# Scores with the keys on the partitions, exp straight from PSUM without the row maximum, row sums from a ones column beside V, and a flagged general path

## The chip, the cores and the metric

One core of one Trainium2 chip runs the program. The metric is device time in microseconds for one execution. TensorE is PE in the profile (PEld is its weight load), VectorE is DVE, ScalarE is ACT, GpSimd is POOL and SyncE is SP.

## The reference

One block of a conditioned transformer: attention with a cached K and V, then a gated MLP that mixes along the sequence. Sizes: 2048 rows, width 512, 32 query heads over 8 K/V heads (4 query heads share one), 2048 keys, head width 128, MLP width 2 x 896.

```python
mod = (silu(c) @ w_mod)                  # six rows of 512: sa, ca, ga, sb, cb, gb
h = layernorm(x) * (1 + ca) + sa
q = h @ wq                               # 32 heads of 128
scores = q k^T * 128 ** -0.5             # per head 2048 x 2048
o = softmax(scores) @ v
x = x + ga * (o @ wo)
h = layernorm(x) * (1 + cb) + sb
z = gelu(h @ w_in)                       # z1 = z[:, :896], z2 = layernorm(z[:, 896:])
g = w_sp @ z2 + b_sp                     # along the sequence, w_sp is 2048 x 2048
x = x + gb * ((z1 * g) @ w_out)
```

The inputs are normal numbers times 0.05; `wq` is scaled down once more by 512 ** -0.5.

## The kernel before

**Set-up (L82 to L219).** SP issues every load: x, c, w_mod and, for each K/V head g, `wq`, V, K and `wo` (`load_group`, L129). 24 columns and two rows of the modulation are made with small matmuls (L163, L189). Everything of K, V, `wq` and `wo` stays in SBUF. K is turned on PE (`kbuild`, L103).

**Attention (L221 to L389).** The loops run over 16 query tiles j of 128 rows, 8 heads g and 4 query heads hh: 512 steps. `prepare_qtile` (L224) normalizes and turns one query tile, `qproj` (L252) makes the four heads' queries of a group with 16 matmuls of 128 columns. A step has two halves:

- `stage1` (L273). Queries on the partitions: four matmuls 128x512 make a row block of scores 128 x 2048 in two PSUM tiles `s_ps` (L280). DVE scales each half out of PSUM into `s_sb` in bf16 and takes the row maximum on the way (L287), then joins the two maxima (L297). ACT takes the exp of the whole 128 x 2048 block with the negated maximum as bias and gives the row sum (L300); DVE inverts it (L309). Then the block of probabilities must have its keys on the partitions, so SP issues one DMA transpose of 128 x 2048 (L321): `pT3`.
- `stage2` (L324), one step later: 16 matmuls of 128 columns with `pT3` as the weights and V as the moving operand (L327), ACT scales the result by the inverse sum (L335), PE turns it (L336).

After the four heads, `group_end` (L338) multiplies by `wo` with four matmuls of 512 columns (L343); after the eight groups, `qtile_end` (L351) adds into x and takes the statistics of the second layer norm. The order is written out by hand with `pending` (L361 on): the next group's `qproj`, then `stage1` of a step, then `stage2` of the step before.

**MLP.** The first half (L437 on) goes by row tile: normalize, turn on PE (L455), shift and scale on ACT (L460), 16 matmuls of 448 columns (L470), then GELU as six instructions on ACT and DVE with a sigmoid (L478 to L499), and statistics (L503). In the same loop SP issues 16 DMA transposes of `w_sp` (L447). When all statistics are there, z2 is normalized (L519). The second half (L531 on) goes by row tile: 32 matmuls of 448 columns (L535), bias on ACT (L543), product on DVE (L551), 7 turns on PE (L559), 7 matmuls with `w_out` (L564), two DVE instructions (L572, L574) and the store (L575).

Of the kernel before, what the change touches and what calls it, by code (L numbers as in the profile page):

```python
# [10 lines left out]
BF16 = mybir.dt.bfloat16  # L11
FP32 = mybir.dt.float32
ACT = mybir.ActivationFunctionType
ALU = mybir.AluOpType
AX = mybir.AxisListType
P = 128
LN_EPS = 1e-5
# [3 lines left out]
def _f_chunk(f: int) -> int:  # L21
    for cand in range(512, 0, -1):
        if f % cand == 0:
            return cand
    return 1


@with_exitstack
def kernel(
    ctx: ExitStack,  # L30
    tc: tile.TileContext,
    A_x: bass.AP,
# [9 lines left out]
    c: bass.AP,  # L42
    w_mod: bass.AP,
    out: bass.AP,
    stage: str = "full",
):
    nc = tc.nc
    _, S, D = A_x.shape
    _, HKV, SK, DH = A_k_cache.shape
    HQ = A_wq.shape[1] // DH  # L50
    REP = HQ // HKV
    F = B_w_in.shape[1]
    FH = F // 2
    NMOD = w_mod.shape[1]
    assert DH == P and D % P == 0 and S % P == 0 and SK % 1024 == 0 and FH % P == 0
    assert D <= 512 and NMOD == 6 * D and REP * P <= 512
    NT = S // P
    NDT = D // P
    NKT = SK // P
    NKH = SK // 1024  # L60
    NFT = FH // P
    FC = _f_chunk(FH)
    NFHC = FH // FC
    NFC = 2 * NFHC
    inv_sqrt_dh = 1.0 / math.sqrt(DH)
    NPE_STEPS = 0

    x_dram = A_x[0].rearrange("(t p) d -> p t d", p=P)
    out_dram = out[0].rearrange("(t p) d -> p t d", p=P)
# [22 lines left out]
    with tc.tile_pool(name="psum_att", bufs=1, space=bass.MemoryType.PSUM) as psum_att, tc.tile_pool(  # L92
        name="attres", bufs=1
# [6 lines left out]
        mv1 = attres.tile([P, NT, nc.vector.BN_AGGR_DIM], FP32, name="mv1")  # L100
# [20 lines left out]
        with tc.tile_pool(name="setup", bufs=1) as setup:  # L121
            wmod_sb = setup.tile([P, NDT, NMOD], BF16, name="wmod_sb")
            c_bf = setup.tile([P, NDT], BF16, name="c_bf")
# [24 lines left out]
            c_f = setup.tile([P, NDT], FP32, name="c_f")  # L148
            nc.vector.tensor_copy(out=c_f[:], in_=c_bf[:])
            sig = setup.tile([P, NDT], FP32, name="sig")  # L150
            nc.scalar.activation(out=sig[:], in_=c_f[:], func=ACT.Sigmoid)
            sc = setup.tile([P, NDT], FP32, name="sc")
            nc.vector.tensor_tensor(out=sc[:], in0=c_f[:], in1=sig[:], op=ALU.mult)
            sc_bf = setup.tile([P, NDT], BF16, name="sc_bf")
            nc.vector.tensor_copy(out=sc_bf[:], in_=sc[:])
            ones_bf = setup.tile([P, P], BF16, name="ones_bf")
            nc.vector.memset(ones_bf[:], 1.0)
            for i in range(6):
                for dt in range(NDT):
                    col = i * NDT + dt  # L160
                    mc_ps = psum_att.tile([P, D], FP32, name="X_ps")
                    for kt in range(NDT):
                        nc.tensor.matmul(  # L163
                            mc_ps[:, 0:1],
                            lhsT=wmod_sb[:, kt, i * D + dt * P : i * D + (dt + 1) * P],
                            rhs=sc_bf[:, kt : kt + 1],
                            start=(kt == 0),
                            stop=(kt == NDT - 1),
                        )
                    nc.vector.tensor_copy(out=modc[:, col : col + 1], in_=mc_ps[:, 0:1])  # L170
            for i in (1, 4):
                nc.vector.tensor_scalar_add(
                    out=modc[:, i * NDT : (i + 1) * NDT],
                    in0=modc[:, i * NDT : (i + 1) * NDT],
                    scalar1=1.0,
                )
            lhs_list = []
            for kt in range(NDT):
                lhs_bc = setup.tile([P, P], BF16, name=f"lhs_bc{kt}")
                nc.vector.tensor_scalar_mul(  # L180
                    out=lhs_bc[:], in0=ones_bf[:], scalar1=sc[:, kt : kt + 1]
                )
                lhs_list.append(lhs_bc)
            for row_out, i in ((ga_rows, 2), (gb_rows, 5)):
                for nch in range((D + 511) // 512):
                    nsz = min(512, D - nch * 512)
                    mr_ps = psum_att.tile([P, D], FP32, name="X_ps")
                    for kt in range(NDT):
                        nc.tensor.matmul(  # L189
                            mr_ps[:, :nsz],  # L190
                            lhsT=lhs_list[kt][:],
                            rhs=wmod_sb[:, kt, i * D + nch * 512 : i * D + nch * 512 + nsz],
                            start=(kt == 0),
# [26 lines left out]
        with tc.tile_pool(name="qpool", bufs=2) as qpool, tc.tile_pool(  # L220
# [130 lines left out]
            def qtile_end(X_ps, j):  # L351
                xa = qpool.tile([P, D], FP32, name="xa")
                nc.vector.tensor_tensor(out=xa[:], in0=X_ps[:], in1=ga_rows[:], op=ALU.mult)
                nc.vector.tensor_tensor(out=x_sb[:, j, :], in0=xa[:], in1=x_sb[:, j, :], op=ALU.add)
                stats2 = qpool.tile([P, 1, nc.vector.BN_STATS_DIM], FP32, name="stats2")
                nc.vector.bn_stats(out=stats2[:, 0, :], in_=x_sb[:, j, :])
                nc.vector.bn_aggr(out=mv2[:, j, :], in_=stats2[:])
                if stage == "attn":
                    nc.sync.dma_start(out=out_dram[:, j, :], in_=x_sb[:, j, :])

            pending = None  # L361
            for j in range(NT):
# [27 lines left out]
            stage2(pg, phh, ppT3, prinv, poT_view)  # L390
            group_end(pX_ps, pg, poT_view)
            qtile_end(pX_ps, pj)

    if stage == "attn":
        return

    with tc.tile_pool(name="mres", bufs=1) as mres:
        win_sb = mres.tile([P, NDT, F], BF16, name="win_sb")
# [176 lines left out]
                nc.sync.dma_start(out=out_dram[:, tt, :], in_=yout[:])  # L575


# [1 line left out]
_INS = ['A_x', 'A_k_cache', 'A_v_cache', 'A_wq', 'A_wo', 'B_x', 'B_w_in', 'B_w_sp', 'B_b_sp', 'B_w_out', 'c', 'w_mod']  # L579
_OUTS = [((1, 2048, 512), 'bfloat16')]  # L580
# [25 lines left out]
```

## Time and profile before

| | |
|---|---|
| median of 3 runs | 2018.55 us (2013.92 to 2029.61) |
| span of the profiled execution, first to last instruction | 2017.7 us |
| median less that span | 0.9 us |
| PE busy, share of the span | 1548.8 us, 77% |
| DVE busy | 1531.4 us, 76% |
| ACT busy | 1384.9 us, 69% |
| DMA queue of SP: share of 16 engines | 83.6% |
| packets on it | 1149168, 303.77 MB |
| read from HBM | 24.78 MB |

The profile comes from one execution. For the profiled execution no time is listed beside its span, so the span stands for it. "Busy" of PE counts pipelined matmuls whose ends are modelled: the distance from the start of one line to the start of the next says more than the mean duration. A group line gives its source line, engine, operation and tile, the shapes, the count, busy time and mean of one instruction, then the idle time of the engine just before and what ended it. A line of the timeline gives start, length, engine, source line, operation, tiles and count; several equal instructions in a row are merged. SPq lines are issues of transfers; their length is the time that the issuing takes.

### The profile page before, as it was taken

What the parts mean: (1) busy time and instruction counts of PE and PEld (TensorE: products, weight loads), DVE (VectorE), ACT (ScalarE), POOL (GpSimd) and SP (SyncE); (2) the same over time, 40 slices, a digit from 0 to 9 for tenths busy, and PEclk for the clock granted to TensorE, in tenths of its full rate; (3) what the DMA queues carried; (4) which work ended last, traced back from release to release, by engine and by line L of the source; (5) the groups of instructions that cost most, each with busy time, mean ns of one, the idle gap of its engine ahead of it and who ended that gap; (6) DMA issues with size and microseconds to landing.
All of it is one profiled execution on the core that took longest, in us unless ns stands there. A gap on an engine that the chain in (4) does not pass through costs nothing. (4 is left out here: it accounts for less than half of the span.)

```text
span 2017.7 us, 36999 instructions
## 1 busy us (share of the span) xinstructions
PE 1548.8 (77%) x14664; PEld 958.1 (47%) x14664; DVE 1531.4 (76%) x3634; ACT 1384.9 (69%) x1804; POOL 1.2 (0%) x8
## 2 busy tenths in 40 slices
PE   4478788878777877777777777777777787756898
PEld 2355455545444545445454555445544554423344
DVE  5478888888878887888777887887888887769422
ACT  1467778777777777777777776777777787768222
POOL 0000000000000000000000000000000000000000
PEclk9799999999999999999989999998999999989899
DMA  9989989999989998999989998988999999990000
GB/s 300 226 142 159 168 161 171 169 160 165 163 152 163 169 162 157 163 157 159 157 142 162 165 160 139 172 151 149 166 158 164 159 173 151 168 209 13 11 17 16
DMA packets 1149342, 306.13 MB, mean 152 GB/s; under 512 B 1134448, under 2 KB 1147632, under 8 KB 1149168
## 3 DMA queue, kind: packets, MB, share of 16 engines
q1 hardware_dynamic: 1149168, 303.77, 83.6%
q8 instruction: 114, 1.87, 0.3%
q14 instruction: 60, 0.49, 0.1%
HBM read 24.78 MB, written 2.10 MB: 13 GB/s over the span
## 5 line engine op out<-in xcount | busy, mean ns | idle before, releaser
L287 DVE TENSOR_SCALAR_CACHE_REDUCE s_sb<-s_ps 128x1024 bf16<-128x1024 f32 x1024 | 1228.4, 1217 | 288.9 <-PE s_ps L280 261.8
L300 ACT ACTIVATE p_sb<-s_sb,nm 128x2048 bf16<-128x2048 bf16 x512 | 1021.7, 1996 | 110.6 <-DVE nm L297 37.1
L327 PE MATMUL o_ps<-v_sb,pT 128*128 128x128 bf16 x8192 | 561.8, 223 | 281.3 <-DMA pT<-p_sb 279.3
L327 PEld LDWEIGHTS <-pT 128*128 128x128 bf16 x8192 | 485.7, 100 | 422.1 <-DMA pT<-p_sb 394.6
L280 PE MATMUL s_ps<-kT_sb,qT 128*128 128x512 bf16 x2048 | 613.6, 388 | 58.9 <-DVE s_sb L287 55.2
L335 ACT ACTIVATE onorm<-o_ps,rinv 128x128 bf16<-128x128 f32 x512 | 184.6, 361 | 322.2 <-PE o_ps L327 320.4
L280 PEld LDWEIGHTS <-qT 128*128 128x128 bf16 x2048 | 178.4, 100 | 131.5 <-issue 78.6
L258 PE MATMUL qT_ps<-hT,wq_sb 128*128 128x128 bf16 x2048 | 174.9, 220 | 5.4 <-ACT qT L266 4.4
L258 PEld LDWEIGHTS <-wq_sb 128*128 128x128 bf16 x2048 | 139.1, 98 | 60.8 <-issue 17.2
L336 PE MATMUL oT_ps<-ident,onorm 128*128 128x128 bf16 x512 | 117.0, 229 | 38.0 <-ACT onorm L335 27.6
L336 PEld LDWEIGHTS <-onorm 128*128 128x128 bf16 x512 | 49.8, 97 | 191.6 <-ACT onorm L335 179.9
L343 PE MATMUL X_ps<-wo_sb,oT 128*128 128x512 bf16 x512 | 135.2, 387 | 2.1 <-DVE oT L340 1.1
L535 PE MATMUL g_ps<-z_sb,wspT_sb 128*128 128x448 bf16 x512 | 103.8, 356 | 12.9 <-DVE z_sb L519 12.9
L300 ACT ACTIVATION_READ_ACCUMULATOR p_sb<-s_sb,nm 128x1 f32 x512 | 96.8, 189 | 0.0
L309 DVE RECIPROCAL rinv<-rs 128x1 f32<-128x1 f32 x512 | 80.9, 158 | 12.1 <-ACT p_sb L300 9.3
L266 ACT ACTIVATE qT<-qT_ps 128x512 bf16<-128x512 f32 x128 | 75.6, 590 | 20.9 <-PE s_ps L280 11.0
L287 DVE DVE_READ_ACCUMULATOR s_sb<-s_ps 128x1 f32 x1024 | 84.4, 82 | 0.0
L340 DVE COPY oT<-oT_ps 128x512 bf16<-128x512 bf16 x128 | 53.9, 421 | 32.8 <-PE oT_ps L336 32.2
L535 PEld LDWEIGHTS <-wspT_sb 128*128 128x128 bf16 x512 | 49.6, 98 | 59.7 <-issue 15.9
L343 PEld LDWEIGHTS <-oT 128*128 128x128 bf16 x512 | 46.2, 99 | 63.6 <-DVE oT L340 16.9
L297 DVE TENSOR_REDUCE nm<-mh 128x1 f32<-128x2 f32 x512 | 73.5, 143 | 3.6
L470 PE MATMUL zpre_ps<-win_sb,h2T 128*128 128x448 bf16 x256 | 53.5, 364 | 28.3 <-ACT xs L478 27.9
(121 smaller groups left out, 481.6 us busy)
## 6 DMA issues: line engine op xcount, KB each, us to landing
pT<-p_sb SPq DMA_TRANSPOSE x512, 4.5
wq_sb<-in_A_wq_dram SPq DMA_DIRECT2D x8, 512.0 KB, 5.9
v_sb<-in_A_v_cache_dram SPq DMA_DIRECT2D x8, 512.0 KB, 7.3
kT_sb<-in_A_k_cache_dram SPq DMA_DIRECT2D x8, 512.0 KB, 8.5
wo_sb<-in_A_wo_dram SPq DMA_DIRECT2D x8, 512.0 KB, 6.0
x_sb<-in_A_x_dram SPq DMA_DIRECT2D x1, 2048.0 KB, 8.4
wmod_sb<-in_w_mod_dram SPq DMA_DIRECT2D x1, 2048.0 KB, 9.3
out_dram<-yout SPq DMA_DIRECT2D x16, 128.0 KB, 1.7
```

The source lines that it names most:

```text
L258: nc.tensor.matmul(qT_view[:, hh, :], lhsT=wq_sb[:, dt, h * DH : (h + 1) * DH], rhs=hT[:, dt, :], start=(hh == 0 and dt == 0), stop=(hh == ...
L266: nc.scalar.activation(out=qT[:], in_=qT_view, func=ACT.Copy)
L280: nc.tensor.matmul(s_ps[:, c2 * 512 : (c2 + 1) * 512], lhsT=qT[:, hh, :], rhs=kT_sb[:, g, kc * 512 : (kc + 1) * 512], start=True, stop=True,)
L287: nc.vector.tensor_scalar(out=s_sb[:, hf * 1024 : (hf + 1) * 1024], in0=s_ps[:], scalar1=inv_sqrt_dh, scalar2=None, op0=ALU.mult, op1=ALU.max,
L297: nc.vector.tensor_reduce(out=nm[:], in_=mh[:], axis=AX.X, op=ALU.max, negate=True)
L300: nc.scalar.activation(out=p_sb[:], in_=s_sb[:], func=ACT.Exp, bias=nm[:], scale=1.0, accum_out=rs[:],)
L309: nc.vector.reciprocal(out=rinv[:], in_=rs[:])
L327: nc.tensor.matmul(o_ps[:], lhsT=pT3[:, kt, :], rhs=v_sb[:, g, kt, :], start=(kt == 0), stop=(kt == NKT - 1),)
L335: nc.scalar.activation(out=onorm[:], in_=o_ps[:], func=ACT.Copy, scale=rinv[:])
L336: nc.tensor.transpose(oT_view[:, hh, :], onorm[:], ident[:])
L343: nc.tensor.matmul(X_ps[:], lhsT=oT[:, hh, :], rhs=wo_sb[:, h, :], start=(h == 0), stop=(h == HQ - 1),)
L535: nc.tensor.matmul(g_ps[:, ch, :FC], lhsT=wspT_sb[:, st, tt * P : (tt + 1) * P], rhs=z2_sb[:, st, ch * FC : (ch + 1) * FC], start=(st == 0 ...
```

## The change

The old kernel function becomes `general_path`, unchanged but for a debugging switch. A new one runs first:

- **Units.** Four chunks of 512 rows, in each the 8 groups; a unit is one group for 128 rows of queries, all four heads together: 128 units. K, V, `wq` and `wo` of a group are loaded a group ahead into double buffers, so each comes from HBM four times. K is turned by a DMA transpose on its way in.
- **Scores turned.** The weights are a block of 128 keys, the moving operand is the 4 x 128 queries of the unit: a matmul 128x512 gives 128 keys by 512 scores. Two of them fill one `s_ps`, 128 x 1024 in fp32, of which there are two.
- **No maximum.** ACT takes the exp from PSUM into `pT` in bf16, which has its keys on the partitions already. No DVE instruction stands between.
- **Sums.** V has a column of ones (`v1`, 130 wide, 129 used); 16 matmuls of 129 columns give a head's output and its sum. DVE inverts the sums and scales two heads at a time.
- **Output.** One DMA transpose 128 x 512 per unit turns the four heads' outputs for `wo`.
- **Order.** `for it`: eight slots; in each the scores of unit `it` (two matmuls), the products with V of unit `it-1` (eight), and one matmul of `qproj` for the next group (slots 0 to 3) or of `wo` for unit `it-2` (slots 4 to 7).
- **MLP.** GELU is one ACT instruction; z1 is made transposed; the mixing works on turned blocks, 16 matmuls of 512 columns per block, so nothing is turned on PE. `w_sp` is loaded with 64 DMA transposes of 512 x 128, the first 32 issued right ahead of the units.
- **Flag.** If an inverse sum lies outside 2^-60 to 2^60, a flag is set; at the end every engine reads it, and `general_path` runs only if it is not zero.

The set-up's queue order is as the diff has it: SP also carries c and the first four tiles of x ahead of the K turns. `ln1_norm` issues four DMA transposes on SP; after `mod_columns` of the last four parts come the two rows ga and gb (8 matmuls of 512 columns). In the MLP each chunk of 512 rows has 32 matmuls of 448 columns and 28 of 512, each group of four followed by one GELU, and later 7 x 16 with `w_sp` and 4 x 7 with `w_out`.

The diff, cut to its core (`general_path` is the kernel shown above):

```diff
+    def load_wsp(t):
+        for st in range(NT):
+            nc.sync.dma_start_transpose(
+                out=wsp[t][:, st, :],
+                in_=B_w_sp[t * 512 : (t + 1) * 512, st * P : (st + 1) * P],
+            )
...
+        def load_group(n):
...
+            g = n % HKV
+            kT = kvp.tile([P, SK], BF16, name="kT")
+            nc.sync.dma_start_transpose(out=kT[:], in_=A_k_cache[0, g])
+            v1 = kvp.tile([P, NKT, DV], BF16, name="v1")
+            nc.gpsimd.memset(v1[:, :, DH:DV], 1.0)
+            nc.gpsimd.dma_start(out=v1[:, :, 0:DH], in_=v_dram[:, g])
...
+            nc.gpsimd.dma_start(out=wo_g[:], in_=wo_dram[:, g * REP : (g + 1) * REP, :])
+            groups[n] = dict(kT=kT, v1=v1, wo=wo_g)
...
+            nc.scalar.dma_start(out=wmod_sb[:, :, 0 : 2 * D], in_=wmod_dram[:, :, 0 : 2 * D])
+            wqs[0] = load_wq(0)
+            load_group(0)
+            nc.scalar.dma_start(
+                out=wmod_sb[:, :, 2 * D : NMOD], in_=wmod_dram[:, :, 2 * D : NMOD]
+            )
+            wqs[1] = load_wq(1)
+            load_group(1)
+            for t in range(1, NCH):
+                nc.sync.dma_start(
+                    out=x_sb[:, t * CT : (t + 1) * CT, :],
+                    in_=x_dram[:, t * CT : (t + 1) * CT, :],
+                )
+            nc.sync.dma_start(out=win_sb[:], in_=win_dram)
+            nc.sync.dma_start(out=wout_sb[:], in_=wout_dram)
+            nc.sync.dma_start(out=bsp_bc[:], in_=B_b_sp.partition_broadcast(P))
...
+            mod_columns((0, 1))
...
+            ln1_mod(0, ln1_norm(0))
...
+            for hh in range(REP):
+                for f in qproj(0, hh):
+                    f()
+
+            mod_columns((2, 3, 4, 5))
...
+        for t in range(2):
+            wsp[t] = wspp.tile([P, NT, 512], BF16, name=f"wsp{t}")
+            load_wsp(t)
...
+        def qk(u, i):
...
+            s_ps = psum.tile([P, 1024], FP32, name="s_ps", bufs=2)
+            for h in range(2):
+                kt = 2 * i + h
+                nc.tensor.matmul(
+                    s_ps[:, h * 512 : (h + 1) * 512].rearrange("p (r q) -> p r q", r=REP),
+                    lhsT=groups[n]["kT"][:, kt * P : (kt + 1) * P],
+                    rhs=qTs[n][:, :, jj * P : (jj + 1) * P],
+                    start=True,
+                    stop=True,
+                )
+            nc.scalar.activation(
+                out=pTs[u][:, 2 * i : 2 * i + 2, :],
+                in_=s_ps[:].rearrange("p (k q) -> p k q", k=2),
+                func=ACT.Exp,
+                scale=inv_sqrt_dh,
+            )
...
+            for kt in range(part * NKT // per, (part + 1) * NKT // per):
+                nc.tensor.matmul(
+                    o_ps[:, hh % 2, 0 : DH + 1],
+                    lhsT=pTs[u][:, kt, hh * P : (hh + 1) * P],
+                    rhs=groups[n]["v1"][:, kt, 0 : DH + 1],
+                    start=(kt == 0),
+                    stop=(kt == NKT - 1),
+                )
...
+                nc.vector.reciprocal(out=rall[:, c0 : c0 + 2], in_=o_ps[:, :, DH])
+                nc.vector.tensor_tensor(
+                    out=onorms[u][:, hh - 1 : hh + 1, :],
+                    in0=o_ps[:, :, 0:DH],
+                    in1=rall[:, c0 : c0 + 2].unsqueeze(2).to_broadcast([P, 2, DH]),
+                    op=ALU.mult,
+                )
...
+            if i == NSLOT - 1:
+                oTs[u] = small.tile([P, REP, P], BF16, name="oT")
+                nc.sync.dma_start_transpose(
+                    out=oTs[u][:], in_=onorms[u][:].rearrange("p r d -> p (r d)")
+                )
...
+            qf = qproj(n + 1, jj) if it < NU and n + 1 < NCH * HKV else []
+            wf = wo_proj(it - 2) if it >= 2 and it - 2 < NU else []
+            for i in range(NSLOT):
+                for fn in later.pop((it, i), []):
+                    fn()
+                if it < NU:
+                    qk(it, i)
+                if 1 <= it <= NU:
+                    pv(it - 1, i)
+                if i < 4 and qf:
+                    qf[i]()
+                if i >= 4 and wf:
+                    wf[i - 4]()
...
+        nc.tensor.matmul(f_ps[:], lhsT=bad[:], rhs=ones_c[:], start=True, stop=True)
+        nc.vector.tensor_copy(out=flag[:], in_=f_ps[:])
...
+                        out=z2[:, j, hf * FC : (hf + 1) * FC],
+                        in_=z_ps[:, :FC],
+                        func=ACT.Gelu_apprx_tanh,
+                    )
...
+                g_ps = psum_m.tile([P, 512], FP32, name="g_ps", bufs=2)
+                for st in range(NT):
+                    nc.tensor.matmul(
+                        g_ps[:],
+                        lhsT=z2[:, st, f * P : (f + 1) * P],
+                        rhs=wsp[t][:, st, :],
+                        start=(st == 0),
+                        stop=(st == NT - 1),
+                    )
...
+    redo = nc.values_load(flag[0:1, 0:1], min_val=0, max_val=P)
+    with tc.If(redo != 0):
+        general_path(
+            tc, A_x, A_k_cache, A_v_cache, A_wq, A_wo, B_x, B_w_in, B_w_sp, B_b_sp, B_w_out,
+            c, w_mod, out,
+        )
```

More of the change, by code (lines that the diff above doesn't have):

```diff
@@ L28, with general_path @@
 @with_exitstack
-def kernel(
+def general_path(
     ctx: ExitStack,
@@ L44 @@
     out: bass.AP,
-    stage: str = "full",
 ):
@@ L357, in qtile_end @@
                 nc.vector.bn_aggr(out=mv2[:, j, :], in_=stats2[:])
-                if stage == "attn":
-                    nc.sync.dma_start(out=out_dram[:, j, :], in_=x_sb[:, j, :])
             pending = None
@@ L392 @@
             qtile_end(pX_ps, pj)
-    if stage == "attn":
-        return
     with tc.tile_pool(name="mres", bufs=1) as mres:
```

418 lines of the change are left out of this document (added).

## The prediction, made before any run

> **What bounds the kernel now.** I read the page first, then the busy time by stretches, then the waits, then the timeline around single steps. The first 50 us, one stretch inside the attention, and the first and last of the MLP:
>
> ```profile
> core 0: us, PE busy (x) PEld busy (x) DVE busy (x) ACT busy (x) POOL busy (x), PEclk, DMA share, GB/s
> 0.00:50.00 50.00, 20.20 (x202) 13.14 (x203) 27.12 (x92) 8.87 (x12) 0.70 (x6) 1.00 1.04 300
> ...
> 1000.00:1200.00 200.00, 157.75 (x1558) 100.78 (x1556) 159.11 (x384) 147.01 (x194) 0.00 (x0) 0.96 0.92 157
> ...
> 1760.00:1800.00 40.00, 21.39 (x133) 11.55 (x134) 16.89 (x33) 18.82 (x31) 0.50 (x2) 0.79 0.85 193
> ...
> 1865.00:2017.00 152.00, 134.42 (x736) 64.94 (x736) 46.38 (x79) 34.99 (x36) 0.00 (x0) 0.94 0.04 14
> ```
>
> No engine is full in the attention, but the DMA engines are, at 0.92. What they carry, and who waits:
>
> ```profile
> PEld L327 <- DMA pT<-p_sb: 394.6, 338, 20.6
> ...
> pT<-p_sb SPq DMA_TRANSPOSE x512, 4.5
> wspT_sb<-in_B_w_sp_dram SPq DMA_TRANSPOSE x16, 4.6
> ```
>
> 512 turns of 128x2048 in bf16, 512 KB each. The second group's queries start here, and the last products with V at 1764.5 us (row below):
>
> ```profile
> 41.40 0.77 PE L258 MATMUL qT_ps<-hT,wq_sb 128*128 128x128 bf16 x11 [0.69 <-ACT qT L266]
> ```
>
> 512 steps in 1723 us are 3.37 us a step, of which a turn fills 0.92 x 3.37 = 3.1 us of all DMA engines. The longest wait of all is that of PE's weight load for a turn. DVE is next, at 0.80 of the stretch. The costs of a step, and the rows that I use for prices below:
>
> ```profile
> L287 DVE TENSOR_SCALAR_CACHE_REDUCE s_sb<-s_ps 128x1024 bf16<-128x1024 f32 x1024 | 1228.4, 1217 | 288.9 <-PE s_ps L280 261.8
> L300 ACT ACTIVATE p_sb<-s_sb,nm 128x2048 bf16<-128x2048 bf16 x512 | 1021.7, 1996 | 110.6 <-DVE nm L297 37.1
> L327 PEld LDWEIGHTS <-pT 128*128 128x128 bf16 x8192 | 485.7, 100 | 422.1 <-DMA pT<-p_sb 394.6
> L266 ACT ACTIVATE qT<-qT_ps 128x512 bf16<-128x512 f32 x128 | 75.6, 590 | 20.9 <-PE s_ps L280 11.0
> L478 ACT ACTIVATE xs<-zpre_ps 128x1792 bf16<-128x1792 f32 x16 | 26.6, 1660 | 14.4 <-PE zpre_ps L470 11.3 <-issue 1.9 <-DVE z_sb L499 0.8
> L353 DVE TENSOR_TENSOR xa<-X_ps,ga_rows 128x512 f32<-128x512 f32 x16 | 11.0, 689 | 2.7 <-PE X_ps L343 2.7
> ```
>
> **What goes.** All 512 turns, all 1024 DVE evacuations (1.23 ms busy) and their maxima. So both of the fullest resources of the attention lose their load, and the question is what PE and ACT then need.
>
> **PE in the attention.** The means of the page are latencies. The pace is the distance between starts of lines that follow without a gap:
>
> ```profile
> 1003.93 1.07 PE L327 MATMUL o_ps<-v_sb,pT 128*128 128x128 bf16 x16 [1.29 <-DMA pT<-p_sb]
> 1004.84 0.81 PE L280 MATMUL s_ps<-kT_sb,qT 128*128 128x512 bf16 x3
> 1005.49 0.72 PE L258 MATMUL qT_ps<-hT,wq_sb 128*128 128x128 bf16 x10
> ```
>
> 16 of 128 columns: 0.91 us, 57 ns each, though each has a 100 ns weight load of its own, so the loads are hidden. Three of 512: 0.65 us, 217 ns each. In proportion 448 take 190. The 129th column adds under 1%, I keep 57; how an odd width reads is not shown, and I take it as free. A slot of the new loop is two score matmuls, one filler and eight products: 3 x 217 + 8 x 57 = 1107 ns. The whole loop: 2048 for scores, 496 `qproj` (all groups but the first), 512 `wo`, so 3056 x 0.217 = 663 us, and 8192 x 0.057 = 467 us: 1130 us.
>
> **ACT in the attention.** One exp of 128x1024 from PSUM per slot. Two copies from PSUM, 512 and 1792 wide, give (1660 - 590) / 1280 = 0.836 ns a column, so 1024 cost 1018 ns. Four in a row start closer than they last:
>
> ```profile
> L460 ACT ACTIVATE h2T<-xn2T_ps,modc 128x128 bf16<-128x128 bf16 x64 | 24.1, 461 | 2.1 <-PE xn2T_ps L455 1.8 <-PE zpre_ps L470 0.4
> ...
> 1785.81 1.50 ACT L460 ACTIVATE h2T<-xn2T_ps,modc 128x128 bf16<-128x128 bf16 x4
> ```
>
> (1.50 - 0.461) / 3 = 346 ns apart, 115 less than one lasts. Lower bound 0.90 us a slot. Upper bound from the exp itself: 1996 - 1024 x 0.836 = 1140 ns, which still has a bias pointer in it that the new one lacks. I take 0.95, nearest to the copies. That is under PE's 1107, so PE sets the slot; `s_ps` has two buffers, an exp starts some 0.65 us into its slot (0.81 - 0.217 for two score matmuls, and a hand-over), ends 1.0 us later and has until 2.2 us: 0.5 us to spare. If this cover fails, the slot is the second rival.
>
> **DVE and POOL.** Per unit one 512-wide evacuation, one 512-wide add, two scalings and two inversions: at most 6 x 0.69 = 4.1 us of 8.9. Hidden. POOL's small tensor instructions have no row (its memsets take 0.2 us); they stand a whole unit ahead, except in the tail.
>
> **DMA in the attention.** Per unit a turn of 128 KB, a quarter of K's 512 KB turn, and 3 x 512 / 4 = 384 KB of plain loads at the 300 GB/s of the first row: 0.78 + 0.78 + 1.3 = 2.8 us of 8.9. The output turn is issued when a unit's products end and is due four and a half slots later, 5.3 us; with 1 us of DVE ahead of it, 4.3 us are left, and four times the data land in 4.5. Zero, with up to 2 us for each of the 32 K turns that share SP's queue as the high end.
>
> **SP's queue at the start of the units.** 32 turns of `w_sp` stand ahead of the first output turn.
>
> ```profile
> 1784.66 32.08 SPq L447 DMA_TRANSPOSE wspT_sb<-in_B_w_sp_dram  x14
> ```
>
> 2.3 us per 512 KB. By size the 128 KB ones take 0.57, 18 us in all, and `wo` of unit 0 is due 23 us in: no stall. If the time belongs to the issue, 73 us: a stall of 50. I take 5, near the first.
>
> **The set-up.** The sizes of the loads are those of before, such as
>
> ```profile
> x_sb<-in_A_x_dram SPq DMA_DIRECT2D x1, 2048.0 KB, 8.4
> ...
> win_sb<-in_B_w_in_dram SPq DMA_DIRECT2D x1, 1792.0 KB, 7.2
> ```
>
> SP's queue takes 2 MB of x, two K turns, `w_in`, `w_out` and b_sp (6.2 MB) before the four turns of the first layer norm; ACT's queue 3 MB and POOL's 3 MB share the engines: 12.2 MB at 300 GB/s, 41 us. Behind it PE works at half pace:
>
> ```profile
> 32.45 0.24 PE L163 MATMUL X_ps<-sc_bf,wmod_sb 128*128 128x1 bf16 x4 [0.25 <-DVE modc L170]
> 32.94 1.87 PE L189 MATMUL X_ps<-wmod_sb,lhs_bc 128*128 128x512 bf16 x4 [0.25 <-DVE modc L170]
> ...
> L189 PE MATMUL X_ps<-wmod_sb,lhs_bc 128*128 128x512 bf16 x8 | 3.7, 620 | 0.9 <-ACT ga_rows L196 0.7 <-DVE modc L170 0.2
> ```
>
> 512 columns cost (1.87 - 0.62) / 3 = 0.42 us here. Turns 2, shift and scale 1.3, 16 `qproj` matmuls 6.8, 64 columns at 0.06 make 4, 8 row matmuls 3.4, hand-overs 1: first scores at 60 us. Low end 45 (before, the second `qproj` runs at 41.4), high end 72, since loads issued by POOL have no row.
>
> **Clock.** After a long PE idle the clock is at half: 0.79 over 40 us and 0.94 over 152 us lose 8 and 9 us. Two restarts (first scores, MLP): 8 each.
>
> **Hand-over to the MLP.** The last unit goes products, scaling, turn, `wo`, sum, statistics, POOL, normalize, turn, shift, then the flag's small matmul, which waits for DVE and has the whole MLP behind it on PE. Before:
>
> ```profile
> 1764.51 1.07 PE L327 MATMUL o_ps<-v_sb,pT 128*128 128x128 bf16 x16 [0.54 <-DMA pT<-p_sb]
> 1766.78 1.89 PE L343 MATMUL X_ps<-wo_sb,oT 128*128 128x512 bf16 x4 [0.52 <-DVE oT L340]
> 1773.96 1.01 PE L455 MATMUL xn2T_ps<-ident_m,xn 128*128 128x128 bf16 x8 [5.29 <-DVE xn L439]
> ```
>
> 9.5 us there without a turn; two turns of up to 4.5 us make 18. Low end 12.
>
> **MLP.** 128 matmuls of 448 at 0.190 and 112 + 448 + 112 of 512 at 0.217: 24 + 146 = 170 us, against 248 us from 1766 to the end. GELU per chunk of 15 groups costs ACT about 15 x 0.5 = 7.5 us under PE's 12. It is PE-bound (the last stretch of before has PE busy in 134 of 152 us), so no more is added.
>
> **End.** Last sums and store, then a branch over the general path, of which no row tells. Before, the last DVE instruction was
>
> ```profile
> 2014.42 0.69 DVE L574 TENSOR_TENSOR yout<-tmp,x_sb 128x512 bf16<-128x512 f32 x1
> ```
>
> and from its start to the end of the span took 3.3 us. I take 7, from 3 to 15.
>
> **The sum.** 60 + 8 + 1130 + 5 + 18 + 8 + 170 + 7 = 1406 us of span, against 2017.7; the median lies 0.9 above the old span, so 1407.
>
> **Rivals.**
> 1. PE sets the slot: 1407; with start 45 to 72, tail, queue and end at their bounds, 1370 to 1450. Chance 0.62.
> 2. ACT sets the slot. At the upper price without overlap and 20 ns of hand-over a slot is 1.16 us: 1024 x 0.053 = 54 more, 1461. For it: only two `s_ps`, and the exp's own row. Against it: 0.95 by the copies. 0.15.
> 3. Turns late on SP's queue: 50 at the start, or 2 us x 32: 1457 to 1510. For it: the median turn before took 4.5 us to land. 0.12.
> 4. The weight loads show. If each product cost the 100 ns of its load, 8192 x 0.043 = 352 more, 1759. Against it: 16 loads and 16 matmuls in 0.91 us above. 0.05. The Trainium skill, TensorE: Matmul & The Clock Gate, section Back-to-back issue gap, holds that load and matmul together set the pace, about 81 ns at 128 columns; by it the sum would be 1604; the 57 ns of this trace speak against it.
> 5. The flag is set and the general path runs as well: 1407 + 2018 = 3425, slower. One place, the branch at the end; it decides once a sum over 2048 exps leaves 2^60, a score near 34. The inputs are normals of 0.05 with `wq` scaled down again, so scores lie near 0 and sums near 2048 = 2^11. 0.02.
> 6. Start and tail both shorter than their low ends: 1350. 0.03. The last 0.01 is for several of these together near the old time.
>
> **How the numbers follow.** Cases 1 to 3 hold 0.89; the range reaches over them, 1360 to 1510. A measurement here tells about 1% from no change. Faster 0.97, within 1% 0.01, slower 0.02.
>
> **What would show it.** Right: some 128 units of 8.9 us; PE's starts 217 and 57 ns apart with no idle from ACT in the units; DMA share near a third; ACT near 0.85; DVE under 0.4; first score at 45 to 72; an MLP of about 170 us. Wrong: PE idle released by the exp (case 2), by `oT` (3), products 80 to 100 ns apart (4), instructions of the general path in the trace (5).

## The result, and the profile after

The median fell from 2018.31 us (2013.92 to 2029.61, 4 runs) to 1535.08 us (1525.00 to 1537.63, 4 runs): a ratio of 0.7588, 95% interval 0.7550 to 0.7626. The direction was as predicted, the size was not: 1407 us was the forecast and 1510 the end of its range. The page of the changed kernel (its lines are: L874 scores, L881 exp, L898 products with V, L815 `qproj`, L918 the turn of a unit's output, L928 `wo`, L649 the turns of `w_sp`, L692 V's load, L694 `wo`'s load, L689 K's turn):

```profile
span 1535.8 us, 27625 instructions
...
PE 1348.6 (88%) x11955; PEld 875.5 (57%) x12169; DVE 467.3 (30%) x1153; ACT 1081.1 (70%) x1087; POOL 123.7 (8%) x229
...
PE   0639999999989989998998999989999998879997
...
PEclk9969999999999999999999999999999999989999
...
L881 ACT ACTIVATE pT<-s_ps 128x1024 bf16<-128x1024 f32 x1024 | 1044.6, 1026 | 285.2 <-PE s_ps L874 214.8
...
oT<-onorm SPq DMA_TRANSPOSE x128, 3.8
```

PE is now the fullest engine, but not full; ACT waits for PE's scores, not PE for the exp; and a turn of 128 KB takes 3.8 us to land in the median. The stages of the sum are read from the timeline: first scores, last products with V, the flag's small matmul, the last DVE instruction.

```profile
59.83 0.59 PE L874 MATMUL s_ps<-qT,kT 128*128 128x512 bf16 x2
...
1341.35 0.63 PE L898 MATMUL o_ps<-v,pT 128*128 128x129 bf16 x8
...
1355.17 0.16 PE L1047 MATMUL f_ps<-ones_c,bad 128*1 128x1 bf16 x1 [7.36 <-DVE bad L1041]
...
1529.91 0.69 DVE L1144 TENSOR_TENSOR yout<-tmp,x_sb 128x512 bf16<-128x512 f32 x1 [1.44 <-DMA out_dram<-yout]
```

| stage | predicted, us | measured, us |
|---|---|---|
| to the first scores | 60 | 59.8 |
| loop, with its restart and SP's queue | 8 + 1130 + 5 = 1143 | 1342.0 - 59.8 = 1282.2 |
| hand-over to the MLP | 18 | 13.2 |
| MLP, with its restart | 178 | 174.7 |
| end | 7 | 5.9 |

The whole excess lies in the loop. Who waits there, in the list of waits:

```profile
PEld L928 <- DMA oT<-onorm: 118.9, 65, 25.7
...
PE misc L928 <- DMA oT<-onorm: 85.4, 42, 25.5
...
PE s_ps L874 <- DMA oT<-onorm: 23.8, 12, 3.0
...
PE s_ps L874 <- ACT pT L881: 2.0, 6, 0.9
```

The columns are total, times and longest. PE waits 2.0 us for the exp in the whole run; it waits for the output turns, once for 25.5 us. That longest wait starts on SP's queue:

```profile
60.07 42.06 SPq L649 DMA_TRANSPOSE wsp<-in_B_w_sp_dram  x32
102.23 1.21 SPq L918 DMA_TRANSPOSE oT<-onorm  x1
```

The 32 `w_sp` turns take 42.06 / 32 = 1.31 us of SP each, and the first output turn stands behind them. A unit in which nothing is late lasts 8.92 us from its first score matmul to the next unit's; the third unit lasts 36.8, 27.9 more. The other loss is spread. One second unit of a group, PE, SP and POOL together:

```profile
600.04 1.16 POOL L692 DMA_DIRECT2D v<-in_A_v_cache_dram  x1 [0.35 <-issue]
...
600.62 0.59 PE L874 MATMUL s_ps<-qT,kT 128*128 128x512 bf16 x2
600.75 1.20 SPq L918 DMA_TRANSPOSE oT<-onorm  x1
...
601.05 0.63 PE L898 MATMUL o_ps<-v,pT 128*128 128x129 bf16 x8
...
601.52 0.38 PE L815 MATMUL misc<-hT,wq_g 128*128 128x512 bf16 x1
...
601.73 0.59 PE L874 MATMUL s_ps<-qT,kT 128*128 128x512 bf16 x2
...
604.39 0.63 PE L898 MATMUL o_ps<-v,pT 128*128 128x129 bf16 x8
...
607.01 0.39 PE L928 MATMUL misc<-wo_g,oT 128*128 128x512 bf16 x1 [1.99 <-DMA oT<-onorm]
```

From 600.62 to 601.73 is one slot, 1.11 us as predicted. The unit starts at 599.50. The turn is issued 1.25 us later, 0.7 us after V's load, and PE needs it when the eight products that start at 604.39 are through, at 604.86: 4.1 us after its issue. It takes 6.2. Taking 8.92 from each unit's length, units 3 to 126 (counted from 0) lose 110.7 us in all, by their place in the group of four:

| unit of the group | load issued shortly before its turn | the turn lands after, median us | lost over 31 units, us |
|---|---|---|---|
| first | K's turn, on SP's queue | 2.86 | 6.7 |
| second | V | 6.27 | 84.6 |
| third | `wo` | 4.24 | 12.6 |
| fourth | none | 2.42 | 6.7 |

K's turn is issued 1.8 us ahead of the first unit's output turn:

```profile
590.08 1.71 SPq L689 DMA_TRANSPOSE kT<-in_A_k_cache_dram  x1
```

Of the 110.7 us, 80 are gaps of PE, and nearly all of these end with an output turn. Most of the rest is the clock: in 15 stretches of 3.4 us, each of which begins within 1.3 us of the end of a gap of 1.8 us or longer, the granted clock stands at 0.50, and half of those 51 us is lost. Over 1080 us of the loop it is 0.98, in a kernel without these waits 1.00 (both rows further down).

With both losses taken off, the loop is 1282.2 - 27.9 - 110.7 = 1143.6 us. That this meets the 1143 of the prediction is in part luck. The 5 us of SP's queue belong to a loss that is taken off, and the 8 us of a restart did not come at the first scores, where the granted clock was 1.00 (50 to 80 us). In their place eight products take 0.47 us, 59 ns each and not 57, some 14 us over all 8192.

### The profile page after: what moved, and what is told of

Read it like the earlier page. It is cut to its first block, busy times and chain, and to the rows that moved or that the text cites. A ratio compares the mean times of both kernels' runs of the same rounds, so it can differ in the third digit from the quotient of the medians.

```text
span 1535.8 us, 27625 instructions
## 1 busy us (share of the span) xinstructions
PE 1348.6 (88%) x11955; PEld 875.5 (57%) x12169; DVE 467.3 (30%) x1153; ACT 1081.1 (70%) x1087; POOL 123.7 (8%) x229
## 3 DMA queue, kind: packets, MB, share of 16 engines
q8 instruction: 97, 1.59, 0.4%
## 4 chain that ended last, share of the span: by engine, by line
PE 66%; DMA 22%; DVE 5%; SPq 4%; issue 1%; ACT 1%; POOL 1%; DVEq 0%; POOLq 0%; ACTq 0%
PE s_ps L874 22%; PE o_ps L898 22%; DMA oT<-onorm 20%; PE misc L928 6%; PE g_ps L1113 6%; PE misc L815 3%; SPq L649 3%; DMA xnT<-xn 2%; PE z_ps L1065 2%; SPq L689 2%; PE z_ps L1085 2%; DVE xacc L941 1%; PE o_ps L1134 1%; DVE onorm L910 1%; DVE bnst L673 1%
## 5 line engine op out<-in xcount | busy, mean ns | idle before, releaser
L881 ACT ACTIVATE pT<-s_ps 128x1024 bf16<-128x1024 f32 x1024 | 1044.6, 1026 | 285.2 <-PE s_ps L874 214.8
L898 PEld LDWEIGHTS <-pT 128*128 128x128 bf16 x8192 | 570.0, 99 | 251.2 <-issue 15.8
L898 PE MATMUL o_ps<-v,pT 128*128 128x129 bf16 x8192 | 657.7, 223 | 0.1
L874 PE MATMUL s_ps<-qT,kT 128*128 128x512 bf16 x2048 | 620.9, 385 | 35.4 <-DMA oT<-onorm 23.8
L874 PEld LDWEIGHTS <-kT 128*128 128x128 bf16 x2048 | 199.9, 98 | 124.3 <-issue 8.2
L928 PE MATMUL misc<-wo_g,oT 128*128 128x512 bf16 x406 | 159.4, 394 | 85.9 <-DMA oT<-onorm 85.4
L815 PE MATMUL misc<-hT,wq_g 128*128 128x512 bf16 x420 | 158.6, 386 | 13.3 <-DVE hT L795 13.2
L928 PEld LDWEIGHTS <-oT 128*128 128x128 bf16 x512 | 51.4, 101 | 120.1 <-DMA oT<-onorm 118.9
L910 DVE TENSOR_TENSOR onorm<-o_ps,rall 128x256 bf16<-128x256 f32 x256 | 106.2, 415 | 0.2
L1113 PE MATMUL g_ps<-wsp,z 128*128 128x512 bf16 x440 | 96.9, 379 | 0.4
L823 DVE CAST qT<-misc 128x512 bf16<-128x512 f32 x128 | 88.2, 689 | 9.6 <-PE misc L815 4.8
L815 PEld LDWEIGHTS <-wq_g 128*128 128x128 bf16 x512 | 50.9, 100 | 17.6 <-issue 17.2
L694 POOL DMA_DIRECT2D wo_g<-in_A_wo_dram x32 | 24.6, 770 | 305.2 <-PE misc L928 198.6
L692 POOL DMA_DIRECT2D v<-in_A_v_cache_dram x32 | 37.5, 1172 | 6.5 <-issue 6.5
```

Source lines behind the costliest of these rows:

```text
L692: nc.gpsimd.dma_start(out=v1[:, :, 0:DH], in_=v_dram[:, g])
L815: nc.tensor.matmul(q_ps[:], lhsT=wqs[n][:, dt, hh * DH : (hh + 1) * DH], rhs=hTs[ch][:, dt, :], start=(dt == 0), stop=(dt == NDT - 1),)
L823: nc.vector.tensor_copy(out=qTs[n][:, hh, :], in_=q_ps[:])
L874: nc.tensor.matmul(s_ps[:, h * 512 : (h + 1) * 512].rearrange("p (r q) -> p r q", r=REP), lhsT=groups[n]["kT"][:, kt * P : (kt + 1) * P], ...
L881: nc.scalar.activation(out=pTs[u][:, 2 * i : 2 * i + 2, :], in_=s_ps[:].rearrange("p (k q) -> p k q", k=2), func=ACT.Exp, scale=inv_sqrt_dh,)
L898: nc.tensor.matmul(o_ps[:, hh % 2, 0 : DH + 1], lhsT=pTs[u][:, kt, hh * P : (hh + 1) * P], rhs=groups[n]["v1"][:, kt, 0 : DH + 1], start=( ...
```

## The experiments

My theory (A): turns on SP's queue come late, at the start behind the issue of the `w_sp` turns and later because the same DMA engines carry V's and `wo`'s loads; the rest of the loop is PE's. Rivals: other queues or stages make up the difference; K's turns on the same queue (my high end); V holds the turn for its many pieces, in HBM or in SBUF. All medians in us; "second unit" is the loss and the turn's median landing as in the table above. For the kernels with the aligned pitch (320 bytes), the loss is left out, because their undisturbed unit is not 8.92.

| kernel | median | ratio to the old kernel, 95% interval | second unit: lost, turn lands |
|---|---|---|---|
| changed kernel | 1535.08 | 0.7588 [0.7550, 0.7626] | 84.6, 6.27 |
| the same again | 1536.32 | 0.7588 [0.7558, 0.7618] | 79.8, 6.09 |
| `wo` a unit later | 1429.44 | 0.7064 [0.7042, 0.7085] | 8.4, 5.99 |
| `w_sp` after the units | 1515.52 | 0.7490 [0.7464, 0.7515] | 81.7, 6.33 |
| both | 1424.41 | 0.7057 [0.7033, 0.7080] | 8.4, 6.29 |
| `wo` later, larger `w_sp` turns | 1408.99 | 0.6979 [0.6956, 0.7002] | 8.0, 6.00 |
| 30 V loads left out | 1455.22 | one run | -0.5, 2.41 |
| 30 K turns left out | 1521.00 | one run | 75.2, 6.24 |
| V in 4 KB runs in HBM | 1536.11 | 0.7623 [0.7590, 0.7656] | 84.6, 6.18 |
| V's rows 320 bytes apart | 1517.38 | 0.7496 [0.7450, 0.7541] | -, 6.12 |
| V in 4 KB rows in SBUF too | 1456.24 | 0.7200 [0.7155, 0.7244] | 2.8, 3.96 |
| V after the turn, first try | 1537.60 | 0.7612 [0.7564, 0.7660] | 78.1, 6.30 |
| V after the turn | 1464.42 | 0.7238 [0.7203, 0.7273] | 0.5, 2.42 |
| no branch | 1492.41 | one run | 54.0, 5.68 |
| no branch, four runs | 1497.27 | 0.7397 [0.7364, 0.7429] | 58.3, 5.87 |
| branch with a small body | 1498.74 | 0.7406 [0.7378, 0.7433] | 61.6, 5.86 |
| branch over matmuls only | 1522.66 | 0.7530 [0.7482, 0.7577] | 77.1, 6.06 |
| `wo` later, larger turns, 320 bytes | 1396.85 | 0.6902 [0.6871, 0.6934] | -, 6.14 |

**More slack for the turn.** `wo` of a unit goes three units behind its scores, its load a unit later.

```diff
-            wf = wo_proj(it - 2) if it >= 2 and it - 2 < NU else []
+            wf = wo_proj(it - 3) if it >= 3 and it - 3 < NU else []
```

> The multiplication by wo is taken three units after the scores instead of two, so the turned output has 13 us instead of 4 us from its issue to its use; wo of the next group is loaded one unit later so that its buffer is free. Theory (the units lose time because PE stands in order behind wo while the output turn lands 5 to 8 us after its issue): every unit takes 8.92 us, the 111 us that units 3 to 127 lose above that vanish, the stall of 28 us in unit 2 shrinks by one unit to 19: 1415 us, 1400 to 1430. Rival (SP's queue as a whole is late, so that one unit of slack only moves the wait): at least 1500.

The second unit's turn lands as late as before (5.99 us) and costs 8.4 in place of 84.6 us. What stays is the start, now in the fourth unit, on PE's timeline:

```profile
105.61 0.61 PE L934 MATMUL misc<-wo_g,oT 128*128 128x512 bf16 x1 [18.79 <-DMA oT<-onorm]
```

**The `w_sp` turns behind the units.** `load_wsp(0)` and `load_wsp(1)` are moved behind the loop.

> The 32 turns of w_sp that stood ahead of the units on SP are issued after the units, with the other 32; everything else is as in the changed kernel. Theory (each turn holds SP for 1.3 us whatever its size, so the first output turn is issued only at 102 us): unit 2 falls from 36.7 to about 9 us, 28 us less, 1507 us, 1500 to 1520, provided the 64 turns (84 us of issue) stay ahead of the mixing. Rival (they are then late for the mixing instead, or the first V and wo loads cause the stall): 1530 or more.

The third unit falls from 36.8 to 8.21 us, and 20 us are gained, not 28. SP's queue and PE at the end of the loop show where 7 us went:

```profile
1322.48 12.99 SPq L649 DMA_TRANSPOSE wsp<-in_B_w_sp_dram  x10
1335.57 1.21 SPq L964 DMA_TRANSPOSE xnT<-xn  x1
```

```profile
1341.05 6.08 PE L1065 MATMUL z_ps<-win_sb,h2T 128*128 128x448 bf16 x16 [7.01 <-ACT z L1072]
```

The last layer norm's turn now stands behind them: DVE waits 9.6 us for it before it makes `h2T` (at 1338.04), ACT's first GELU waits for that, and PE for ACT. The queue's cost is 1.3 us a turn wherever they are put.

**Both together.**

> wo one unit later and the first 32 w_sp turns after the units, both edits together. Theory (two separate waits, one behind each other's back: the output turns in the units and the 42 us of w_sp issues at their start): of the 30 us that the first edit alone left in the units, the 19 in unit 3 vanish, and the 7 us come back that the second edit alone lost behind the units, where a layer norm's turn stood behind w_sp turns on SP: 1417 us, 1408 to 1425. Rival (the first edit has hidden the start as well): no faster than 1429.

At the upper end of the expected window. The tail's 7 us return with the moved turns, and the loop loses 8.5 us in all. That rest is no late turn: in two second units PE waits 2.8 us ahead of its products for DVE, with a stretch at half the granted clock behind it.

**Fewer, larger turns.** With `wo` later, the 32 turns of 512 x 128 become 16 of 1024 x 128.

```diff
+        for st in range(NT):
+            nc.sync.dma_start_transpose(
+                out=wsp_a[:, st, :], in_=B_w_sp[0:1024, st * P : (st + 1) * P]
+            )
```

> wo one unit later, and the first half of w_sp by 16 turns of 1024 x 128 at the old place instead of 32 of 512 x 128. Theory (an issue holds SP 1.2 to 1.3 us whatever its size up to some 0.5 MB, where K's take 1.8): the turns end some 16 x 1.5 = 24 us after the start, before the first output turn is due at 32 us, no stall in unit 3: 1429 - 20 = 1409 us, 1402 to 1416. Rival (issue time goes with size, as in the prediction's first reading): 42 us again, 1429.

```profile
59.05 22.29 SPq L862 DMA_TRANSPOSE wsp_a<-in_B_w_sp_dram  x16
```

22.29 / 16 = 1.39 us each at twice the size: up to 256 KB SP's time goes nearly with the count. (K's turns of 512 KB take 1.80 us, median.) The busy time, clock (0.98 and 1.00, then DMA share and GB/s) of the loop, first of the changed kernel, then of this one:

```profile
110.00:1190.00 1080.00, 1001.29 (x9506) 679.89 (x9678) 306.36 (x784) 900.49 (x880) 91.47 (x157) 0.98 0.33 71
```

```profile
110.00:1190.00 1080.00, 1063.66 (x10381) 732.05 (x10567) 329.15 (x842) 982.02 (x963) 95.82 (x164) 1.00 0.37 75
```

At 1408.99 us this is the 1407 of the sum: with its turns on time the kernel does what the prediction said.

**Which transfer holds the turn?** In two kernels the first two groups' V, or K, are kept and used for all others, so that 30 of the 32 loads are left out.

```diff
-            v1 = kvp.tile([P, NKT, DV], BF16, name="v1")
+            if n < 2:
+                v1 = keep.tile([P, NKT, DV], BF16, name=f"v1_{n}")
...
+            else:
+                v1 = groups[n - 2]["v1"]
```

> V is loaded only for the first two groups and their tiles are used again in turn, so 30 of 32 loads of V are left out and the output is not the reference's; K turns and wo loads stay. Theory A (the 256-byte rows of V's load share the DMA engines with the output turn of the second unit of each group): the second units fall from 11.6 us to about 9, the output turn lands in 2.4 to 4.2 us there, 1450 us, 1440 to 1470. Theory B (the K turn ahead on SP's queue holds it up): no change, 1525 to 1540. Theory C (a turn takes that long by itself): no change either.

> K is turned only for the first two groups and those tiles are used again in turn, so 30 of 32 K turns are left out and the output is not the reference's; loads of V and wo stay. Theory A (V's load is the cause): 1520 to 1540, the second units still at 11 us or more. Theory B (K turns on SP's queue are the cause): 1430 to 1450. Theory C (a turn takes that long by itself): no change.

Without V's loads the loss of the second unit is gone and the turn's median landing is 2.6 us over all units (first row, from the page's list of transfers); without K's turns PE still waits 99 us for it (second row, from the list of waits). K's turn under way costs the next output turn 0.4 us: in the first unit it lands after 2.86 us with it and 2.42 without.

```profile
oT<-onorm SPq DMA_TRANSPOSE x128, 2.6
```

```profile
PE misc L931 <- DMA oT<-onorm: 99.0, 52, 26.1
```

**Is it when V is under way?** The load is made to follow the turn: one element of the turned output is copied into V's tile first, and the load writes over it.

```diff
+            if n in vgate:
+                nc.gpsimd.tensor_copy(out=v1[0:1, 0, 0:1], in_=oTs[vgate[n]][0:1, 0, 0:1])
             nc.gpsimd.dma_start(out=v1[:, :, 0:DH], in_=v_dram[:, g])
```

In the first try the element went to a tile of its own, and the copy came behind the load on GpSimd's queue; V had not moved, and 1537.60 us is a repetition of the changed kernel.

> V's load waits on GpSimd, by a read of one element, until the output turn of its unit has landed; nothing else is moved by hand. Theory A, only a transfer that is under way at the turn's time holds it: the 80 to 85 us of the second unit go, some 5 to 25 come back at the third, because V now ends later and wo's load stands behind it on GpSimd's queue: 1460 to 1485. Rival 1, wherever V goes the next turn waits for it: 1520 to 1540. Rival 2, V was not the cause and leaving it out helped in another way: 1535.

> V's load again made to wait on GpSimd for the output turn of its unit: one element of the turned output is first copied into V's tile, and the load writes over it. Theory A, only a transfer under way at the turn's time holds it: V is issued some 4.5 us into the second unit, the turn there lands in 2.5 us and its 80 to 85 us go, 5 to 25 come back at the third unit, because V now ends later and wo's load stands behind it: 1455 to 1480. Rival, wherever V goes the next turn waits for it: 1520 to 1540.

```profile
608.30 1.19 SPq L922 DMA_TRANSPOSE oT<-onorm  x1
...
610.81 0.18 POOL L695 COPY v<-oT 1x1 bf16<-1x1 bf16 x1 [3.62 <-DMA oT<-onorm]
...
611.28 1.17 POOL L696 DMA_DIRECT2D v<-in_A_v_cache_dram  x1 [0.30 <-POOL v L695]
...
612.42 0.38 PE L932 MATMUL misc<-wo_g,oT 128*128 128x512 bf16 x1
```

In the timeline of one second unit the turn lands 2.5 us after its issue, PE does not wait, and the load follows. 72 us are gained against the changed kernel run again (1536.32); the third unit's loss grew from 12.6 to 20.8. So it is V's bytes being under way at that moment.

**Why V more than `wo`, with as many bytes?** First the source: 16 neighbouring keys on a partition, so that each partition reads 4 KB in one run (K's columns are then read at a stride of 16).

```diff
-    v_dram = A_v_cache[0].rearrange("g (t p) d -> p g t d", p=P)
+    v_dram = A_v_cache[0].rearrange("g (p t) d -> p g t d", p=P)
```

> Only V's load is changed: a partition takes 16 neighbouring keys, so its rows in memory are 4 KB long instead of 256 bytes, and the score matmul takes every 16th column of K as weights so that the keys agree; all bytes are still loaded, wo stays two units behind. Theory (the many 256-byte packets of V, not its bytes, delay the output turn): in the second units the turn lands in 3 to 4.3 us, what it does beside wo's load with its 1 KB rows, the 85 us there shrink to 10 or less: 1460 us, 1450 to 1475. Rival (the bytes matter): at least 1515. Should weights with a stride of 16 columns load slower than a score matmul hides, each unit is longer by that: visible as units above 8.92 us.

Nothing moved: it is as the rival said. Then the start of the rows in SBUF, `DV = DH + 32` in place of `DH + 2`:

> V's tile has 160 columns per 128 keys in place of 130, so that each of its 256-byte rows in SBUF begins 320 bytes after the last, and not 260. Theory A, rows that begin at odd places are written slowly: V's packets of 4 KB take about 160 ns as those of the weights do, not 252, V lands 4.7 us after its issue, not 6.8, the output turn of a group's second unit lands in some 4.2 us, and of the 85 us lost there about 75 go: 1460, 1445 to 1480. Rival, V is slow for its 256-byte pieces wherever they begin: 1535, 1525 to 1545.

And last rows of 4 KB in SBUF as well:

```diff
+    v_dram = A_v_cache[0].rearrange("g (p t) d -> p g (t d)", p=P)
...
+            v1 = kvp.tile([P, VW + 2], BF16, name="v1")
...
+            nc.gpsimd.dma_start(out=v1[:, 0:VW], in_=v_dram[:, g])
```

> V is loaded as one row of 4096 bytes per partition, in HBM and in SBUF, with 16 neighbouring keys in it; the key weights are read at a stride of 16, which cost nothing before. The ones column stands only behind the last keys and the flag is set to zero by hand, so that the sums are left out and the output is not the reference's; the matmuls keep their number and sizes. Theory B, the 256-byte pieces in SBUF make V's load slow: its packets take 159 ns as those of the weights do, V lands in 4.7 us, the turn of the second unit in 4.3, and that unit's loss falls from 85 to 13 us: 1463, 1450 to 1480. Rival, V's pieces do not matter: 1535, 1520 to 1545.

V's landing in these three, in this order, from the page's list of transfers (the last figure is us from issue to landing):

```profile
v<-in_A_v_cache_dram POOLq DMA_DIRECT2D x32, 512.0 KB, 6.8
```

```profile
v<-in_A_v_cache_dram POOLq DMA_DIRECT2D x32, 512.0 KB, 6.6
```

```profile
v<-in_A_v_cache_dram POOLq DMA_DIRECT2D x32, 512.0 KB, 4.1
```

It is the pieces in SBUF. The packets hold 4 KB in all three; their median time in the trace is some 250 ns with pieces of 256 bytes 260 apart, some 230 with a pitch of 320, and 159, that of `wo` and `wq`, with rows of 4 KB. The guess that the start of the rows decides at a grain of 64 bytes fell: with the pitch of 320 the turn still lands after 6.12 us, and 1517.38 us lies in neither expected window. The Trainium skill, DMA: Bandwidth & Descriptors, section Why small descriptors are slow (HBM only), puts the overhead of a 256-byte descriptor at 27% and holds SBUF-to-SBUF transfers free of it; here the SBUF side alone makes packets more than half as long again (250 / 159), with the HBM side in 4 KB runs. The Trainium skill's section How a descriptor splits into AXI transactions, on the same page, adds that a descriptor which does not start at a multiple of 256 bytes has its first transaction start at the boundary below, so that by this rule 256 bytes would take two and not one. The last kernel changed length and that alignment together, so the runs do not part them.

The pitch of 320 gained 19 us all the same, 128 x 0.11 = 14 of them on PE. Scores, products with V, filler and next scores on this kernel's timeline

```profile
652.50 0.59 PE L874 MATMUL s_ps<-qT,kT 128*128 128x512 bf16 x2
652.93 0.62 PE L898 MATMUL o_ps<-v,pT 128*128 128x129 bf16 x8
653.38 0.38 PE L815 MATMUL misc<-hT,wq_g 128*128 128x512 bf16 x1
653.60 0.59 PE L874 MATMUL s_ps<-qT,kT 128*128 128x512 bf16 x2
```

show 653.38 - 652.93 = 0.45 us for eight products, against 601.52 - 601.05 = 0.47 above, and an undisturbed unit lasts 8.81 us. Put into the kernel with late `wo` and large turns:

> The kernel with the output projection three units behind the scores and half of the w_sp turns twice as large (1409 us), and V's rows 320 bytes apart in place of 260. Theory C, the products with V read rows that begin at multiples of 64 bytes faster, whatever the transfers do: every unit 8.81 us in place of 8.92, 128 times 0.11 less: 1395, 1390 to 1402. Rival, the shorter units came of fewer or shorter late turns: 1409, 1404 to 1414.

1396.85 us, a loop without late turns and 0.11 us less in each unit. It is the fastest kernel here, 9% below the changed one. That a start at multiples of 64 bytes is what makes the rows faster is not shown, and one run speaks against it: in the kernel with 4 KB rows the products read rows 256 bytes apart, and there eight take 0.47 us and an undisturbed unit 8.94.

**The code that never runs.** Leaving out the flag's read, the branch and the general path was meant to price the end, and gained 43 us, in the loop:

> The reading of the flag and the branch over the general path are left out, so that the general path could never run; the flag itself is still made. Theory (the branch costs what the prediction's 7 us of end hold above store and last sums): 2 to 4 us less, 1531 to 1533, from a tail that ends about 2 us after the last store is issued. Rival (the branch and its code cost nothing): 1535; rival (the large code behind it slows the fetch all along): 1500 or less.

> The changed kernel with the read of the flag, the branch and the general path left out, so that it is right only where the flag is zero, timed in rounds. If the branch or the code behind it slows the loads of the loop (the single run of it was 1492 us): 1485 to 1500. If that single run was a chip that happened to be quicker: as the changed kernel on this chip, 1525 to 1545.

> The flag's read and the branch stay, and the general path behind it is replaced by one small fill and one store, so that the kernel is right only where the flag is zero. If the size of the code behind the branch is what slows the loads: as without the branch, 1485 to 1500. If the read and the branch themselves do it: 1535, 1525 to 1545.

> The branch's body is replaced by 17,600 matmuls with their weight loads, as many instructions as the general path has, with one store and no transfers between; the kernel is right only where the flag is zero, and the body never runs. If the amount of code that lies behind the branch slows the loop's transfers: 1535, 1525 to 1545. If it is something else that the general path brings: as with a small body, 1490 to 1505.

The branch itself costs nothing (1498.74 with a small body, 1497.27 without it); the body costs 37.6 us without being run, and 17,600 matmuls with their weight loads in its place some 24 of them, which lies between the two expected windows. As many instructions are recorded but for ten, and the instruction queues carry nearly the same (1.59 + 0.27 MB and 1.56 + 0.22 MB); what differs is how long the loads from HBM take (K's turns too, 4.6 us and 4.0), and the turns beside them. From the page of the changed kernel run again, then from that of the small body:

```profile
span 1535.9 us, 27839 instructions
...
v<-in_A_v_cache_dram POOLq DMA_DIRECT2D x32, 512.0 KB, 6.5
wo_g<-in_A_wo_dram POOLq DMA_DIRECT2D x32, 512.0 KB, 4.7
...
oT<-onorm SPq DMA_TRANSPOSE x128, 4.0
```

```profile
span 1499.8 us, 27829 instructions
...
v<-in_A_v_cache_dram POOLq DMA_DIRECT2D x32, 512.0 KB, 6.4
wo_g<-in_A_wo_dram POOLq DMA_DIRECT2D x32, 512.0 KB, 4.2
...
oT<-onorm SPq DMA_TRANSPOSE x128, 3.2
```

Why the code behind the branch lengthens the loads stays open, and no run parts its amount from where it makes the tensors lie in memory. The 14 us between the general path and the matmuls stay open too; there the intervals overlap. That a few tenths of a microsecond a load are worth this much I put down to the turn beside them, which is already late; this is not shown, since no kernel with late `wo` was run without the general path.

## Why the prediction was right and where it failed

- **PE sets the slot:** right. 1107 ns predicted, 1.11 us measured; the weight loads stay hidden; the exp costs 1026 ns (1018 from the copies), and PE waited 2.0 us for it. The products took 59 ns and not 57. With the turns on time the whole kernel takes 1408.99 us.
- **Set-up, hand-over, MLP, end:** 263 predicted, 253.6 measured. The hand-over was 5 too long, the MLP 3. The general path did not run.
- **"Clock":** two restarts of 8 us were taken. At the first scores none came, since PE had been at work before them at a granted clock of 1.00. At the MLP it was some 2 us: the granted clock was 0.50 until 1360, and PE began there at 1355. What the clock cost in the loop, some 26 us behind late turns, had no term.
- **"DMA in the attention": the step that failed.** It costed the output turns at zero, because 4.3 us were left and "four times the data land in 4.5". The slack was 4.1 us, near enough (the 5.3 us before it are 4.8 slots of 1.107, not four and a half); the landing was the mistake. The 4.5 us came from a kernel in which SP's queue alone fed the engines, and I set mean shares (2.8 us of 8.9) against a question of one moment: what is in flight when the turn is issued. V's load is, and the turn lands after 6.3 us, not 2.4. My high end was put on K's turns, which share the queue and cost at most some 14 us here (1535 to 1521, one run); the plain loads of another queue had no price at all. That is 111 us of the 128, 80 in waits and most of the rest in the half clock behind them. Some of it is not in the change as such but in the code behind the branch (38 us).
- **"SP's queue at the start of the units":** 5 taken, 27.9 measured, between the ends 0 and 50. I divided by size where the time goes nearly by instruction: 1.31 us for 128 KB, 1.39 for 256 KB. The row I had, 2.3 us for 512 KB, gave 0.57 by size and 2.3 by instruction; the measured 1.31 lies between the two, and I stayed near the wrong end.
- **The range:** rival 3 had the right mechanism, late turns, but held its two parts as alternatives, 50 or 64; alone they give 1457 or 1471, and only both together come near its end of 1510 (1407 - 5 + 50 + 64 = 1516). Both came, 28 + 111 = 139 us, and the second by a transfer that I had not named. The bounds listed under rival 1 also add up to something else, 1377 to 1472 and not 1370 to 1450. The measured time lies outside either way.

## What to carry to other kernels

Compare a short transfer's slack with its landing time beside whatever other queues have in flight at its issue, not with its landing time alone or with mean shares of the DMA engines; where the two are close, a unit more of software pipelining (106 us here) is worth more than the best mending of the transfer (79 us, V in 4 KB rows). Count queue time by instructions, and make few large turns of many small ones. Look at the pieces into which a load falls in SBUF, and not only at those in HBM: 4 KB runs in HBM alone changed nothing here.

## What the hardware showed that I had not expected

- A 128 KB output turn lands in 2.4 us alone, 2.9 beside K's turn, 4.2 beside `wo`'s load and 6.3 beside V's, though the DMA engines are busy to a third. The Trainium skill, DMA: Bandwidth & Descriptors, section Issuing engines are not separate DMA queues, says that transfers from all engines run on the same 16 DMA engines and interleave; the turns agree.
- 512 KB lands in 4.1 us as 128 rows of 4 KB and in 6.8 as pieces of 256 bytes in SBUF.
- Moving rows of 129 columns 320 bytes apart are read 3 to 4% faster than 260 or 256 bytes apart (0.45 and 0.47 us for eight).
- In units 3 to 126 PE waited 21 times for 1.8 us or longer, and 15 times its granted clock fell to 0.50 for 3.4 us about the end of such a wait.
- The general path behind a branch that is not taken, 36,999 instructions in its own profile, costs 38 us; 35,200 matmuls and weight loads in its place cost 24.
